# Attention followed by a gated unit: the spatial bias moved from TensorE matmuls to a VectorE add, and the spatial blocks dealt among the blocks of u

## The chip, the cores and the metric

The kernel runs on one core of one Trainium2 chip. Its time is the device time of one execution, in microseconds (us). A core has several engines that run their own instruction streams in order and wait for each other on semaphores. In the profile they are called PE (TensorE, matmuls), PEld (the weight loads of TensorE, which overlap its matmuls), DVE (VectorE), ACT (ScalarE), POOL (GpSimd) and SP (SyncE, which issues most DMAs).

## The reference

Attention with 16 query heads on 4 key heads (batch 8, sequence 384, head size 64) makes x of shape 8 x 384 x 1024. A gated unit follows. All inputs and the output are float32.

```
h = np.maximum(x @ w_in, 0.0)                  # 1024 -> 1024
u, v = h[..., :512], h[..., 512:]
v_n = (v - mean(v)) / np.sqrt(var(v) + 1e-06)  # over the last axis
v_s = np.einsum('ts,bsd->btd', w_spatial, v_n) + b_spatial[None, :, None]
gated = u * v_s
out = gated @ w_out                            # 512 -> 1024
```

The spatial product mixes the 384 positions of the sequence; `b_spatial` has one value for each position t. In the kernel's layout for `v_s` the columns d are on partitions and t runs along the row, so the bias is a row of 384 values that is the same on every partition.

## The kernel before

The work is written out as one order of instructions for each engine. A main loop goes over steps n, 18 for each batch. In a step the attention of batch b is issued: `scores(n)` (tile `sc`, two matmuls of 64 x 512 each, then the exponential on ACT into `aT`) and `weigh` (12 matmuls into `av`, then on DVE the reciprocal `r` and the product `x`, lines 273 and 275; there is one `av` buffer in PSUM, so that each group of `av` waits for the `x` of the one before). DMA loads, casts on POOL and transposes stand in a table `todo` by step. The loads and the transposing DMAs are issued on SP's queue.

Beside the attention of batch b runs the gated unit of batch b-1. `gated_unit(b)` is a Python generator: it issues matmuls and yields their column count after each. `run_fill` takes from it until the columns of this step's share have been issued: `COLS` divided by 18, with `COLS` the columns of one unit (line 397). So PE's order is fixed: in each step attention first, then a share of the unit. The unit of batch b starts at step 18(b+1)+2; that of the last batch (b = 7) runs after all attention, with nothing beside it. "Unit b" below means the call `gated_unit(b)`.

A unit has these parts in order:

- `pv` (line 311): three blocks of 8 matmuls with 512 columns, for the half v. DVE takes each from PSUM with a ReLU (`vr`, line 321), then `stats` and `mv` (lines 323, 324).
- `pu` (line 333): four blocks (m = 0 to 3) of 8 matmuls with 384 columns, for the half u. ACT takes each out with a ReLU as `uT` (line 341). Behind block 0 ACT computes `rstd` (lines 343, 344). Behind block 1 DVE computes `nmr` (line 346) and POOL the three normalised blocks `vn` (line 351), 128 x 512 each.
- `psp` (lines 363 and 366): four spatial blocks. Each starts with one matmul of `ones_b` with `bias_b`, which puts the bias into PSUM (float32 split into two float16 rows, 0 and 32 of `bias_b`; all other rows are zero), then three matmuls with the three `vn`. DVE multiplies the block by `uT` into `gT` (line 374).
- `po` (line 381): six blocks of 4 matmuls with 512 columns; the four take `gT` blocks 0 to 3 as weights in that order. DVE and ACT copy them to `osb` (line 390), SP stores them.

All PSUM blocks of the unit come from one pool, `ps_ck`, with three buffers. The bias is loaded by `load_b` (line 402) and made ready by `prep_spatial` (line 405, three POOL operations on one partition).

Of the kernel before, what the change touches and what calls it, by code (L numbers as in the profile page):

```python
# [9 lines left out]
FP32 = mybir.dt.float32  # L10
FP16 = mybir.dt.float16
AF = mybir.ActivationFunctionType
ALU = mybir.AluOpType
# [4 lines left out]
def kernel(  # L18
# [16 lines left out]
    nc = tc.nc  # L35
    P = 128
    B, HQ, S, D = q.shape
# [3 lines left out]
    DH = DFF // 2  # L41
    NT = S // P
    NB = DM // P
    NM = DH // P
    G = HQ // HKV
    assert (HQ, HKV, S, D, DM, DFF) == (16, 4, 384, 64, 1024, 1024)
    scale = D ** -0.5
# [5 lines left out]
    cst = ctx.enter_context(tc.tile_pool(name="cst", bufs=1))  # L53
# [3 lines left out]
    moe = ctx.enter_context(tc.tile_pool(name="moe", bufs=2))  # L57
# [34 lines left out]
    def load_q0(j, lo, hi, eng):  # L92
# [18 lines left out]
            name=nc.get_next_instruction_name(), act_func_set_id=set_id, ins=[], outs=[]  # L111
# [41 lines left out]
    eps_t = cst.tile([P, 1], FP32, name="eps_t")  # L153
    nc.vector.memset(eps_t, 1e-6)
    v1 = [cst.tile([P, HKV, NT, VW], FP16, name=f"v1_{i}") for i in range(2)]
    for i in range(2):
        nc.gpsimd.memset(v1[i][:, :, :, D:VW], 1.0)
    ones_b = cst.tile([P, P], FP16, name="ones_b")
    nc.gpsimd.memset(ones_b, 0.0)
    nc.gpsimd.memset(ones_b[0:1, :], 1.0)  # L160
    nc.gpsimd.memset(ones_b[32:33, :], 1.0)
    bias_b = cst.tile([P, S], FP16, name="bias_b")
    nc.gpsimd.memset(bias_b, 0.0)


    k16s, q16s = {}, {}
# [115 lines left out]
    def x_tile(b):  # L282
        if b not in xts:
            xts[b] = att.tile([P, NT, NB, P], FP16, name=f"xt_{b}", tag="xt")
        return xts[b]
# [17 lines left out]
    def gated_unit(b):  # L303
        xt = x_tile(b)
        last = b == B - 1
        mv = small.tile([P, NT, 2], FP32, name=f"mv_{b}", tag="mv")
        v_r, v_n = [], []
        for st in range(NT):
            pv = ps_ck.tile([P, 512], FP32, name=f"pv_{b}_{st}", tag="ck")
            for kt in range(NB):  # L310
                nc.tensor.matmul(  # L311
                    pv,
                    xt[:, st, kt],
                    w_in16[:, kt, DH:DFF],
                    start=(kt == 0),
                    stop=(kt == NB - 1),
                )
                if kt < NB - 1:
                    yield 512
            vr = moe.tile([P, DH], FP32, name=f"vr_{b}_{st}", tag="vr", bufs=4)  # L320
            nc.vector.tensor_scalar(vr, pv, 0.0, None, op0=ALU.max)  # L321
            stats = small.tile([P, 6], FP32, name=f"stats_{b}_{st}", tag="stats")
            nc.vector.bn_stats(stats, vr)  # L323
            nc.vector.bn_aggr(mv[:, st, :], stats)
            v_r.append(vr)
            yield 512
        rstd = small.tile([P, NT], FP32, name=f"rstd_{b}", tag="rstd")
        nmr = small.tile([P, NT], FP32, name=f"nmr_{b}", tag="nmr")
        uT = moe.tile([P, NM, S], FP16, name=f"uT_{b}", tag="uT")
        for m in range(NM):  # L330
            pu = ps_ck.tile([P, 512], FP32, name=f"pu_{b}_{m}", tag="ck")
            for kt in range(NB):
                nc.tensor.matmul(  # L333
                    pu[:, 0:S].rearrange("p (t s) -> p t s", t=NT),
                    w_in16[:, kt, m * P : (m + 1) * P],
                    xt[:, :, kt],
                    start=(kt == 0),
                    stop=(kt == NB - 1),
                )
                yield S  # L340
            nc.scalar.activation(uT[:, m, :], pu[:, 0:S], AF.Relu)  # L341
            if m == 0:
                nc.scalar.activation(rstd, mv[:, :, 1], AF.Ln, bias=eps_t)
                nc.scalar.activation(rstd, rstd, AF.Exp, scale=-0.5)
            if m == 1:
                nc.vector.scalar_tensor_tensor(  # L346
                    nmr, mv[:, :, 0], -1.0, rstd, op0=ALU.mult, op1=ALU.mult
                )
                for st in range(NT):
                    vn = moe.tile([P, DH], FP16, name=f"vn_{b}_{st}", tag="vn", bufs=6)  # L350
                    nc.gpsimd.tensor_scalar(  # L351
                        vn,
                        v_r[st],
                        rstd[:, st : st + 1],
                        nmr[:, st : st + 1],
                        op0=ALU.mult,
                        op1=ALU.add,
                    )
                    v_n.append(vn)
        gT = moe.tile([P, NM, S], FP16, name=f"gT_{b}", tag="gT")  # L360
        for m in range(NM):
            psp = ps_ck.tile([P, 512], FP32, name=f"psp_{b}_{m}", tag="ck")
            nc.tensor.matmul(psp[:, 0:S], ones_b, bias_b, start=True, stop=False)  # L363
            yield S
            for st in range(NT):
                nc.tensor.matmul(  # L366
                    psp[:, 0:S],
                    v_n[st][:, m * P : (m + 1) * P],
                    wsT16[:, st, :],
                    start=False,  # L370
                    stop=(st == NT - 1),
                )
                yield S
            nc.vector.tensor_tensor(gT[:, m, :], psp[:, 0:S], uT[:, m, :], ALU.mult)  # L374
        rows = out[b].rearrange("(p t) d -> p t d", t=NT)
        for tt in range(NT):
            osb = ops.tile([P, DM], FP32, name=f"osb_{b}_{tt}", tag="osb")
            for half in range(2):
                po = ps_ck.tile([P, 512], FP32, name=f"po_{b}_{tt}_{half}", tag="ck")
                for m in range(NM):  # L380
                    nc.tensor.matmul(  # L381
                        po,
                        gT[:, m, tt * P : (tt + 1) * P],
                        w_out16[:, m, half * 512 : (half + 1) * 512],
                        start=(m == 0),
                        stop=(m == NM - 1),
                    )
                    yield 512
                cols = slice(half * 512, (half + 1) * 512)
                (nc.scalar.copy if half else nc.vector.tensor_copy)(osb[:, cols], po)  # L390
                if last:
                    nc.sync.dma_start(rows[:, tt, cols], osb[:, cols])
            if not last:
                nc.sync.dma_start(rows[:, tt, :], osb)

    HV = NB * 512
    COLS = NT * HV + NM * NB * S + NM * (NT + 1) * S + NT * 2 * NM * 512


    b32 = cst.tile([1, S], FP32, name="b32")  # L400

    def load_b():
        nc.sync.dma_start(b32, moe_b_spatial.rearrange("(a s) -> a s", a=1))

    def prep_spatial():
        lo32 = cst.tile([1, S], FP32, name="lo32")
        bp = b32.rearrange("a (p t) -> a t p", t=NT)
        hi = bias_b[0:1, :].rearrange("a (t p) -> a t p", t=NT)
        nc.gpsimd.tensor_copy(hi, bp)
        nc.gpsimd.tensor_tensor(lo32.rearrange("a (t p) -> a t p", t=NT), bp, hi, ALU.subtract)  # L410
        nc.gpsimd.tensor_copy(bias_b[32:33, :], lo32)

    def load_ws():
        t = cst.tile([P, NT, S], FP32, name="ws32")
# [53 lines left out]
    at(12, load_w_in, 1, 0)  # L468
    at(13, load_ws)
    at(13, load_b)  # L470
    at(13, load_w_out, 0)
    at(14, k_transposes, 1, 0, by_dve)
# [47 lines left out]
    def run_fill(cols):  # L520
        nonlocal owed
        owed = owed + cols if fill else 0.0
        while fill and owed > 0:
            try:
                owed -= next(fill[0])
            except StopIteration:
                fill.pop(0)

    early = 0
    for n in range(total + 6):  # L530
        for f, args in todo.pop(n, []):
            f(*args)
        if n + 1 < NU:
            scores(n + 1)
        elif n >= NU and n % 2 == 0 and n < total:
            scores(n)
            scores(n + 1)
        for hh in range(2):
            b, r = divmod(n - 3 - hh, NU)
            if n >= 3 + hh and r % 3 == 0 and b < B:  # L540
                weigh(b, r // 3, hh)
        if n == 13:
            fill.append(gated_unit(0))
        if n >= 2 * NU + 2 and (n - 2) % NU == 0 and (n - 2) // NU <= B:
            fill.append(gated_unit((n - 2) // NU - 1))
        if n < NU + 3:
            if 13 <= n and early < 2 * HV:
                c = min(768, 2 * HV - early)
                early += c
                run_fill(c)  # L550
        else:
            run_fill((COLS - (early if n < 2 * NU + 2 else 0)) / (NU if n >= 2 * NU + 2 else NU - 1))
    for g in fill:
# [31 lines left out]
```

## Time and profile before

| What | us |
| --- | --- |
| median of 3 runs | 267.28 |
| lowest, highest | 263.93, 268.06 |
| the profiled execution | 264.56 |
| its span, first to last instruction | 262.6 |
| PE busy | 243.8 |
| ACT busy | 169.0 |
| DVE busy | 143.7 |
| POOL busy | 73.0 |
| 32 bias matmuls, mean of one (with latency) | 0.325 |
| 96 spatial matmuls, mean of one (with latency) | 0.326 |
| gT, mean of one of 32 | 0.556 |

The profile is of one execution. The duration of a matmul there includes its latency; matmuls overlap, and the distance from one start to the next is the time that PE is taken. In the groups of instructions a row gives line, engine, operation, output and inputs with shapes, count, then busy time and mean ns of one, then the idle time of the engine just ahead of them and who ended it. In the timeline a row gives start, duration, engine, line, operation, and a count where neighbours were merged; idle time ahead is in square brackets. In a table of stages a row gives the stretch, its length, busy time of PE, PEld, DVE, ACT and POOL with counts, the granted TensorE clock as a share of full speed, DMA share and GB/s.

### The profile page before, as it was taken

To read this page: it belongs to the slowest core of one execution; us is meant where nothing else is said; L and a number is where in the kernel's file an instruction comes from. 1 tells how busy PE (TensorE), PEld (TensorE's weight loads), DVE (VectorE), ACT (ScalarE), POOL (GpSimd) and SP (SyncE) were. 2 spreads that over 40 slices of the span, in tenths; PEclk is the share of its full clock that TensorE was granted. 3 is DMA by queue.
4 is the path that set the end of the run, shared out by engine and by line. 5 is a ranking of instruction groups with operands and counts; after the bars stand their busy time and mean duration, and the time that the engine had idled before them with its cause. 6 is when DMAs were issued, how large, how long until landed. Compare 5 with 4: busy or idle time off the path is not lost.

```text
span 262.6 us, 5743 instructions
## 1 busy us (share of the span) xinstructions
PE 243.8 (93%) x2325; PEld 123.5 (47%) x2325; DVE 143.7 (55%) x372; ACT 169.0 (64%) x218; POOL 73.0 (28%) x112
## 2 busy tenths in 40 slices
PE   1776879999999999999999999999999998999994
PEld 1343435554455444554455445544455445544551
DVE  3257577455563647374654556364736465465642
ACT  2668346777768675868677776867586865862222
POOL 2446697614103330316013510333030000300120
PEclk9999799999999999999999999999999999999999
DMA  7999798399909995599739990999465340005006
GB/s 188 330 353 353 258 388 262 74 266 252 287 6 204 299 295 69 104 286 284 202 64 200 275 313 21 179 325 224 151 116 113 111 171 2 0 2 240 2 0 240
DMA packets 76715, 49.32 MB, mean 188 GB/s; under 512 B 45969, under 2 KB 70546, under 8 KB 76690
## 3 DMA queue, kind: packets, MB, share of 16 engines
q1 hardware_dynamic: 75650, 48.70, 70.3%
q8 instruction: 18, 0.29, 0.5%
q10 hardware_dynamic: 1040, 0.26, 0.4%
q14 instruction: 7, 0.06, 0.1%
HBM read 25.76 MB, written 12.58 MB: 146 GB/s over the span
## 4 chain that ended last, share of the span: by engine, by line
PE 83%; DVE 6%; DMA 5%; issue 1%; ACT 1%; SPq 1%; POOL 0%; DVEq 0%
PE pu L333 16%; PE av L263 15%; PE po L381 15%; PE pv L311 14%; PE sc L249 13%; PE psp L366 6%; DMA q<-in_q_dram 3%; DMA xt<-x 2%; DVE x L275 2%; PE psp L363 2%; PE xps L291 1%; PE qps L216 1%; DVE w_in L134 1%; DVE r L273 1%; ACT osb L390 1%
## 5 line engine op out<-in xcount | busy, mean ns | idle before, releaser
L256 ACT ACTIVATE aT<-sc 128x1024 f16<-128x1024 f32 x144 | 139.7, 1022 | 64.5 <-PE sc L249 64.4
L263 PEld LDWEIGHTS <-aT 128*128 128x128 f16 x1152 | 44.7, 98 | 33.8 <-issue 7.5
L263 PE MATMUL av<-v,aT 128*128 128x65 f16 x1152 | 53.2, 195 | 4.1 <-DVE x L275 3.8
L273 DVE RECIPROCAL r<-av 128x4 f32<-128x4 f32 x96 | 17.0, 177 | 65.6 <-PE av L263 65.6
L351 POOL TENSOR_SCALAR vn<-vr,rstd,nmr 128x512 f16<-128x512 f32 x24 | 18.2, 773 | 116.5 <-DVE nmr L346 94.3
L311 PE MATMUL pv<-w_in,xt 128*128 128x512 f16 x192 | 47.9, 380 | 0.3 <-DVE osb L390 0.2
L249 PE MATMUL sc<-qT,kT 64*128 64x512 f16 x288 | 46.8, 394 | 1.5 <-ACT aT L256 0.7
L381 PE MATMUL po<-w_out,gT 128*128 128x512 f16 x192 | 47.8, 379 | 0.4 <-ACT osb L390 0.3
L333 PE MATMUL pu<-xt,w_in 128*128 128x384 f16 x256 | 47.8, 326 | 0.0
L275 DVE TENSOR_TENSOR x<-av,r 128x256 f16<-128x256 f32 x96 | 40.7, 424 | 3.3
L188 POOL CAST q<-q 128x768 f16<-128x768 f32 (+1 forms) x32 | 24.8, 803 | 20.0 <-DMA q<-in_q_dram 14.5
L333 PEld LDWEIGHTS <-w_in 128*128 128x128 f16 x256 | 22.9, 97 | 15.5 <-issue 3.0
L311 PEld LDWEIGHTS <-xt 128*128 128x128 f16 x192 | 16.6, 97 | 18.3 <-issue 3.1
L381 PEld LDWEIGHTS <-gT 128*128 128x128 f16 x192 | 16.7, 97 | 16.1 <-DVE gT L374 1.7
L374 DVE TENSOR_TENSOR gT<-psp,uT 128x384 f16<-128x384 f32 x32 | 17.7, 556 | 10.2 <-PE psp L366 9.5
L366 PE MATMUL psp<-wsT,vn 128*128 128x384 f16 x96 | 22.2, 326 | 0.0
L249 PEld LDWEIGHTS <-kT 64*128 64x128 f16 x288 | 9.5, 94 | 26.9 <-issue 24.9
L390 ACT COPY osb<-po 128x512 f32<-128x512 f32 x24 | 14.1, 589 | 12.4 <-PE po L381 12.4
L321 DVE TENSOR_SCALAR vr<-pv 128x512 f32<-128x512 f32 x24 | 16.6, 691 | 9.0 <-PE pv L311 8.3
L341 ACT ACTIVATE uT<-pu 128x384 f16<-128x384 f32 x32 | 15.6, 493 | 9.0 <-PE pu L333 9.0
L390 DVE COPY osb<-po 128x512 f32<-128x512 f32 x24 | 16.5, 687 | 6.1 <-PE po L381 6.0
L323 DVE BATCH_NORM_STATS2 stats<-vr 128x6 f32<-128x512 f32 x24 | 16.7, 694 | 0.8
(45 smaller groups left out, 105.3 us busy)
## 6 DMA issues: line engine op xcount, KB each, us to landing
q<-in_q_dram SPq DMA_DIRECT2D x14, 768.0 KB, 7.9
out_dram<-osb SPq DMA_DIRECT2D x21, 512.0 KB, 3.9
wi<-in_moe_w_in_dram SPq DMA_DIRECT2D x4, 1024.0 KB, 9.4
v<-in_v_dram SPq DMA_DIRECT2D x8, 384.0 KB, 9.0
k<-in_k_dram SPq DMA_DIRECT2D x7, 384.0 KB, 4.6
wo<-in_moe_w_out_dram SPq DMA_DIRECT2D x2, 1024.0 KB, 6.9
out_dram<-osb SPq DMA_DIRECT2D x6, 256.0 KB, 2.0
q<-in_q_dram SPq DMA_DIRECT2D x2, 512.0 KB, 7.6
```

The source lines that it names most:

```text
L188: eng.tensor_copy(q16s[b, j][:, lo:hi, :, hh, :], src[:, hh, lo:hi])
L249: nc.tensor.matmul(sc[:, hh], kTs[b][half, j, t * P : (t + 1) * P], qTs[b, j][half, qt], start=True, stop=True,)
L256: nc.scalar.activation(aTs[b, m][:, t], sc, AF.Exp, scale=scale)
L263: nc.tensor.matmul(av[:, i, :], aTs[b, m][:, t, hh, i * P : (i + 1) * P], v1[b % 2][:, 2 * j + hh, t, 0 : D + 1], start=(t == 0), stop=(t ...
L273: nc.vector.reciprocal(r, av[:, :, D : D + 1])
L275: nc.vector.tensor_tensor(x16s[b][:, qt, blk : blk + 2].rearrange("p k (i d) -> p (k i) d", i=2), av[:, :, 0:D], r.to_broadcast([P, G, D]) ...
L311: nc.tensor.matmul(pv, xt[:, st, kt], w_in16[:, kt, DH:DFF], start=(kt == 0), stop=(kt == NB - 1),)
L333: nc.tensor.matmul(pu[:, 0:S].rearrange("p (t s) -> p t s", t=NT), w_in16[:, kt, m * P : (m + 1) * P], xt[:, :, kt], start=(kt == 0), stop ...
L351: nc.gpsimd.tensor_scalar(vn, v_r[st], rstd[:, st : st + 1], nmr[:, st : st + 1], op0=ALU.mult, op1=ALU.add,)
L366: nc.tensor.matmul(psp[:, 0:S], v_n[st][:, m * P : (m + 1) * P], wsT16[:, st, :], start=False, stop=(st == NT - 1),)
L381: nc.tensor.matmul(po, gT[:, m, tt * P : (tt + 1) * P], w_out16[:, m, half * 512 : (half + 1) * 512], start=(m == 0), stop=(m == NM - 1),)
L390: (nc.scalar.copy if half else nc.vector.tensor_copy)(osb[:, cols], po)
```

## The change

The bias is loaded to all 128 partitions and kept as float32 (`bias_bc`). A spatial block has only its three matmuls. DVE first adds the bias to the block from PSUM into a float32 tile `vs` in SBUF, and multiplies `vs` by `uT` into `gT` with a second operation. The order of the blocks changes: u 0, u 1, the normalisation (`normal`), u 2, spatial 0, u 3, spatial 1, 2, 3. `nmr` and `vn` are issued after the yield that follows block 1 of u. `COLS` loses the columns of the bias matmuls: 41472 for 43008, 2304 for 2389 a step.

```diff
-    ones_b = cst.tile([P, P], FP16, name="ones_b")
...
-    bias_b = cst.tile([P, S], FP16, name="bias_b")
-    nc.gpsimd.memset(bias_b, 0.0)
+    bias_bc = cst.tile([P, S], FP32, name="bias_bc")
...
+        def u_block(m):
             pu = ps_ck.tile([P, 512], FP32, name=f"pu_{b}_{m}", tag="ck")
             for kt in range(NB):
...
-                yield S
+                if kt < NB - 1:
+                    yield S
             nc.scalar.activation(uT[:, m, :], pu[:, 0:S], AF.Relu)
...
+            yield S
+
+        def normal():
+            nc.vector.scalar_tensor_tensor(
+                nmr, mv[:, :, 0], -1.0, rstd, op0=ALU.mult, op1=ALU.mult
+            )
+            for st in range(NT):
...
+        def spatial_block(m):
             psp = ps_ck.tile([P, 512], FP32, name=f"psp_{b}_{m}", tag="ck")
-            nc.tensor.matmul(psp[:, 0:S], ones_b, bias_b, start=True, stop=False)
-            yield S
             for st in range(NT):
                 nc.tensor.matmul(
                     psp[:, 0:S],
                     v_n[st][:, m * P : (m + 1) * P],
                     wsT16[:, st, :],
-                    start=False,
+                    start=(st == 0),
                     stop=(st == NT - 1),
                 )
-                yield S
-            nc.vector.tensor_tensor(gT[:, m, :], psp[:, 0:S], uT[:, m, :], ALU.mult)
+                if st < NT - 1:
+                    yield S
+            vs = moe.tile([P, S], FP32, name=f"vs_{b}_{m}", tag="vs")
+            nc.vector.tensor_tensor(vs, psp[:, 0:S], bias_bc, ALU.add)
+            nc.vector.tensor_tensor(gT[:, m, :], vs, uT[:, m, :], ALU.mult)
+            yield S
+
+        yield from u_block(0)
+        nc.scalar.activation(rstd, mv[:, :, 1], AF.Ln, bias=eps_t)
+        nc.scalar.activation(rstd, rstd, AF.Exp, scale=-0.5)
+        yield from u_block(1)
+        normal()
+        yield from u_block(2)
+        yield from spatial_block(0)
+        yield from u_block(3)
+        for m in range(1, NM):
+            yield from spatial_block(m)
...
-    COLS = NT * HV + NM * NB * S + NM * (NT + 1) * S + NT * 2 * NM * 512
+    COLS = NT * HV + NM * NB * S + NM * NT * S + NT * 2 * NM * 512
...
-    b32 = cst.tile([1, S], FP32, name="b32")
+    b32 = cst.tile([P, S], FP32, name="b32")
...
-        nc.sync.dma_start(b32, moe_b_spatial.rearrange("(a s) -> a s", a=1))
+        nc.sync.dma_start(b32, moe_b_spatial.partition_broadcast(P))
...
-        nc.gpsimd.tensor_tensor(lo32.rearrange("a (t p) -> a t p", t=NT), bp, hi, ALU.subtract)
-        nc.gpsimd.tensor_copy(bias_b[32:33, :], lo32)
+        nc.gpsimd.tensor_copy(
+            bias_bc.rearrange("a (t p) -> a t p", t=NT), b32.rearrange("a (p t) -> a t p", t=NT)
+        )
```

More of the change, by code (lines that the diff above doesn't have):

```diff
@@ L157 @@
         nc.gpsimd.memset(v1[i][:, :, :, D:VW], 1.0)
-    ones_b = cst.tile([P, P], FP16, name="ones_b")
-    nc.gpsimd.memset(ones_b, 0.0)
-    nc.gpsimd.memset(ones_b[0:1, :], 1.0)
-    nc.gpsimd.memset(ones_b[32:33, :], 1.0)
-    bias_b = cst.tile([P, S], FP16, name="bias_b")
-    nc.gpsimd.memset(bias_b, 0.0)
+    bias_bc = cst.tile([P, S], FP32, name="bias_bc")
     k16s, q16s = {}, {}
@@ L329, in gated_unit @@
         uT = moe.tile([P, NM, S], FP16, name=f"uT_{b}", tag="uT")
-        for m in range(NM):
+        gT = moe.tile([P, NM, S], FP16, name=f"gT_{b}", tag="gT")
+        def u_block(m):
             pu = ps_ck.tile([P, 512], FP32, name=f"pu_{b}_{m}", tag="ck")
@@ L339, in gated_unit @@
                 )
-                yield S
+                if kt < NB - 1:
+                    yield S
             nc.scalar.activation(uT[:, m, :], pu[:, 0:S], AF.Relu)
[L342 to L347, printed above, removed]
-                )
[L349 to L361, printed above, removed]
+            yield S
[4 more added lines that the diff above has]
+            for st in range(NT):
+                vn = moe.tile([P, DH], FP16, name=f"vn_{b}_{st}", tag="vn", bufs=6)
+                nc.gpsimd.tensor_scalar(
+                    vn,
+                    v_r[st],
+                    rstd[:, st : st + 1],
+                    nmr[:, st : st + 1],
+                    op0=ALU.mult,
+                    op1=ALU.add,
+                )
+                v_n.append(vn)
+        def spatial_block(m):
             psp = ps_ck.tile([P, 512], FP32, name=f"psp_{b}_{m}", tag="ck")
-            nc.tensor.matmul(psp[:, 0:S], ones_b, bias_b, start=True, stop=False)
-            yield S
             for st in range(NT):
@@ L396 @@
     HV = NB * 512
-    COLS = NT * HV + NM * NB * S + NM * (NT + 1) * S + NT * 2 * NM * 512
-    b32 = cst.tile([1, S], FP32, name="b32")
+    COLS = NT * HV + NM * NB * S + NM * NT * S + NT * 2 * NM * 512
+    b32 = cst.tile([P, S], FP32, name="b32")
     def load_b():
-        nc.sync.dma_start(b32, moe_b_spatial.rearrange("(a s) -> a s", a=1))
+        nc.sync.dma_start(b32, moe_b_spatial.partition_broadcast(P))
     def prep_spatial():
[L406 to L409, printed above, removed]
-        nc.gpsimd.tensor_tensor(lo32.rearrange("a (t p) -> a t p", t=NT), bp, hi, ALU.subtract)
-        nc.gpsimd.tensor_copy(bias_b[32:33, :], lo32)
+        nc.gpsimd.tensor_copy(
+            bias_bc.rearrange("a (t p) -> a t p", t=NT), b32.rearrange("a (p t) -> a t p", t=NT)
+        )
     def load_ws():
```

## The prediction

> **What bounds the kernel now.** I read the page's first part for the engines, then busy time by stage, then the groups of the lines that the diff touches, then the timeline of one unit (unit b is the call gated_unit(b); its work on PE is dealt among the attention of batch b+1, and the last unit runs alone), and the granted clock last.
>
> ```profile
> PE 243.8 (93%) x2325; PEld 123.5 (47%) x2325; DVE 143.7 (55%) x372; ACT 169.0 (64%) x218; POOL 73.0 (28%) x112
> ```
> ```profile
> 181.50:210.10 28.60, 28.60 (x278) 14.02 (x276) 15.88 (x41) 20.64 (x28) 2.28 (x3) 1.00 0.54 139
> ```
> The second line is unit 5: length, then PE, PEld, DVE, ACT and POOL busy, clock, DMA. PE is busy all of it, DVE little over half. A busy PE need not be at its peak, so I check by spacing. From its pv at 181.53 to that of unit 6 at 210.11 are 28.58 us. In the last unit 32 pu matmuls take 5.36 us, the last of them 0.33, so one of 384 columns takes (5.36-0.33)/31 = 0.162; 24 pv take 5.34, so one of 512 takes 0.216. Four sc take 0.54 (193.65 to 194.19) and twelve av 0.38 (194.19 to 194.57). A unit has 48 matmuls of 512 (10.4), 32 pu (5.2), 16 psp with the bias (2.6), 9 groups of sc (4.9) and 12 of av (4.6): 27.7 of 28.58. So PE's order of work is the clock of units 0 to 7; about 0.9 us a unit is spare, and a PE wait is added in full.
>
> ```profile
> L351 POOL TENSOR_SCALAR vn<-vr,rstd,nmr 128x512 f16<-128x512 f32 x24 | 18.2, 773 | 116.5 <-DVE nmr L346 94.3
> L374 DVE TENSOR_TENSOR gT<-psp,uT 128x384 f16<-128x384 f32 x32 | 17.7, 556 | 10.2 <-PE psp L366 9.5
> L366 PE MATMUL psp<-wsT,vn 128*128 128x384 f16 x96 | 22.2, 326 | 0.0
> L323 DVE BATCH_NORM_STATS2 stats<-vr 128x6 f32<-128x512 f32 x24 | 16.7, 694 | 0.8
> ```
> The third line is the one to look at: psp never waits for vn today. The timeline of unit 5 shows how closely that is so (start, duration, and idle time in brackets):
>
> ```profile
> 193.65 0.61 PE L249 MATMUL sc<-qT,kT 64*128 64x512 f16 x4
> ...
> 193.88 0.16 DVE L346 SCALAR_TENSOR_TENSOR nmr<-mv,rstd 128x3 f32<-128x3 f32 x1 [0.46 <-ACT rstd L344]
> ...
> 194.19 0.54 PE L263 MATMUL av<-v,aT 128*128 128x65 f16 x12
> 194.22 2.28 POOL L351 TENSOR_SCALAR vn<-vr,rstd,nmr 128x512 f16<-128x512 f32 x3 [13.14 <-DVE nmr L346]
> ...
> 194.57 2.27 PE L333 MATMUL pu<-xt,w_in 128*128 128x384 f16 x13
> 194.77 0.18 DVE L273 RECIPROCAL r<-av 128x4 f32<-128x4 f32 x1 [0.72 <-PE av L263]
> 194.99 0.42 DVE L275 TENSOR_TENSOR x<-av,r 128x256 f16<-128x256 f32 x1
> ...
> 197.85 0.33 PE L363 MATMUL psp<-bias_b,ones_b 128*128 128x384 f16 x1
> ...
> 202.40 0.46 PEld L381 LDWEIGHTS <-gT 128*128 128x128 f16 x3 [0.19 <-DVE gT L374]
> ```
> The three vn end at 196.50, and PE comes to psp at 197.85: 1.35 us of cover, made of pu blocks 2 and 3 with sc and av between. At the other end the last gT of a unit is just in time (0.19).
>
> **The change part by part.**
>
> *Bias matmuls go.* 32 x 0.162 = 5.2 us of PE time, 0.65 a unit, all on the path.
>
> *Where psp block 0 and nmr come to stand.* In the built order of the changed kernel, units 1 to 6 run on PE: 6 pu, sc, av, 8 pu (block 2), 3 psp (block 0), pu block 3 with sc and two av, psp 1 to 3, 2 po, av, 2 po. The fill deals 2304 columns a step, not 2389, and block 1 of u ends with a step; nmr is therefore issued a step later and on DVE stands behind r and x of that av, where before it stood ahead of them. Counted from the av at 194.19 (in the changed kernel it comes 2 pu earlier, which shifts all that follows alike): x ends at 195.41, nmr (0.16) at 195.61, POOL starts 0.18 later as before (194.04 to 194.22), at 195.8, and at 0.765 each the vn end at 196.56, 197.33 and 198.1. PE reaches psp 0 at 194.57 + 8 x 0.162 = 195.87. Its third matmul can start at about 198.15 and not at 196.19: 1.95 us lost. Behind it in PE's queue stand all pu, sc and av; nothing is run in their place. Bounds: 1.75, if x overlaps nmr and nothing passes between the engines; 2.2, if POOL's result takes another 0.2 to reach PE. Six units x 1.95 = 11.7. In unit 0 block 1 ends a matmul before a step's end, so that nmr stays ahead of r, and sc and two av lie between: vn end at 51.6 (49.31 + 2.28), PE reaches psp 0 at about 52.8. Nothing lost there. Unit 6 has the x transposes of the last batch and their copies between; I take it as the others.
>
> *Second DVE operation.* The add reads PSUM and a second operand as gT does: 0.556. The product reads SBUF alone; the nearest row is stats, 694 for 512 elements, so 694 - 128/0.96 = 0.56 for 384. With 0.03 between operations (vr to stats) a block costs 1.18 where it cost 0.59. The Trainium skill, "VectorE: DVE Perf Modes", section on the errata for SBUF-source operations, tables 58 cycles plus one per element from SBUF to SBUF: an estimate of 0.46 us by that page. The row of stats disagrees with it, and the row decides; by the page a unit's three blocks would lose 0.3 us less.
> PE makes psp 1 to 3 with one sc group between, in about 2.1 us; DVE needs 3.5, and r and x (0.63) come first. I continue unit 5 from psp 0's end at 198.3: psp 1 leaves PE at 201.4, psp 3 at 203.05, two po at 203.5, av at 203.85. DVE: vs 1 starts at 201.65, and three pairs end at 202.8, 204.0 and 205.2. The third and fourth po want gT 2 and gT 3; the fourth starts at 205.2 where it could have at 204.1. So 1.1 us lost; bounds 0.7 (product at 0.42, by DVE's cast of q, 290 ns for 256 elements from SBUF) and 1.2 (a gap of 0.06 instead of 0.03). Six units: 6.6. Behind the third pair on DVE stand r and x of that av, and the next av on PE waits for them; the two po and sc between (0.97) cover their 0.65. In unit 0 only one sc group stands between psp 3 and the po: r and x, vs 2, gT 2, vs 3 and gT 3 end about 3 us after psp 3, less sc 0.54 and three po 0.65: 1.9 lost.
>
> *The last unit*, with nothing beside it:
>
> ```profile
> 248.66 2.28 POOL L351 TENSOR_SCALAR vn<-vr,rstd,nmr 128x512 f16<-128x512 f32 x3 [22.20 <-PE pu L333]
> ...
> 252.50 1.86 DVE L374 TENSOR_TENSOR gT<-psp,uT 128x384 f16<-128x384 f32 x3 [0.16 <-PE psp L366]
> ...
> 254.41 4.22 PEld L381 LDWEIGHTS <-gT 128*128 128x128 f16 x21 [0.56 <-DVE gT L374]
> ```
> Block 2 of u ends at 249.62; psp 0 could end at 250.1 and must wait for the third vn (250.94), to 251.2: 1.1 lost. Then u 3 to 252.5 and psp 1 to 253.0, out at 253.15; three pairs on DVE end at 256.5, where the last gT ended at 254.36. The fourth po moves from 254.41 to 256.5: 2.1 later, net of this unit's bias matmuls.
>
> *Costed at nothing:* the load of the bias on 128 rows (hidden by 13 us between its issue and its use; uncovered it would hold unit 0's first add); one POOL copy for three operations of 0.69, 1.01 and 0.50 (POOL next waits 0.75 for q anyway); the memsets, under POOL's first wait for v; SP's new order, where the last x transpose of a batch passes the last store (PE's waits for xt are 0.8 in all, so a gain of at most that). ACT gets the same operations.
>
> *Sum.* -0.65 x 7 + 11.7 + 6.6 + 1.9 + 2.1 = +17.7. The profiled execution took 264.56 (span 262.6, so 2.0 around it): 282.3, **282 us**. Its time lies 2.7 under the median, 267.28, of runs from 263.93 to 268.06; from the median the sum gives 285.0.
>
> **The rivals.**
> *Faster: the waits are hidden.* If nmr ran where it does now, and DVE caught up under the attention, PE keeps the 5.2 us: 259.4. For it: DVE is 55% busy and POOL 28%. Against it: those are averages, and cover between nmr and psp falls from 13 pu, sc and av to 8 pu. It decides if both waits together stay under 0.65 us a unit.
> *Only one wait is real*, say the pairs on DVE (or vn at a third of its size): 282.3 - 8 = about 274. For it: today's 0.19 us is the only wait of this kind. Against: vn's 2.28 us is fixed, and PE's 1.3 us in front of psp 0 can be counted.
> *The clock falls as well.*
>
> ```profile
> 26.00:27.00 1.00, 0.00 (x0) 0.00 (x0) 0.97 (x4) 0.68 (x1) 0.24 (x1) 1.00 1.05 391
> 27.00:28.00 1.00, 0.54 (x13) 0.49 (x14) 0.40 (x1) 0.00 (x0) 0.00 (x0) 1.00 1.04 385
> 28.00:29.00 1.00, 1.00 (x10) 0.55 (x7) 0.91 (x3) 0.00 (x0) 0.93 (x2) 0.71 1.07 406
> 29.00:30.00 1.00, 1.00 (x5) 0.23 (x4) 0.48 (x2) 0.21 (x1) 1.00 (x3) 0.50 0.86 343
> ```
> PE waited 2.17 us, and from about 28.5 to 31.9 the clock was half. Gaps of 0.6 to 0.9 before it did nothing. Each wait for vn is 1.95 us, in three pieces with a psp matmul between. If each cost 3.4 us at half clock, 1.7 us would be lost per unit, 10 in six: 288 with some, 292 with all. The Trainium skill, "TensorE: Matmul & The Clock Gate", section "HAM oscillation — how this bites in real kernels", allows idle gaps up to about 3.4 us, so by that page none would fall; the trace does not agree, since 2.17 was enough. I hold the pieces for enough work, but not safely.
>
> **How the numbers follow.** Forecast 0.70, own range 277 to 287 (bounds of vn: -1.2 to +1.5; of DVE: -2.4 to +0.6; start from 264.56 or from the median). Clock 0.14, at 287 to 294. One wait 0.08, at 272 to 277. Little changed 0.04, faster 0.04. The range, 273 to 290, leaves out the faster cases and the upper half of the clock's. About 2% is what a measurement of this kernel tells from no change: faster 0.04, same 0.06 (with the low end of one wait), slower 0.90.
>
> **What would show it.** The psp group on PE with some 12 us idle, released by POOL vn; weight loads of po waiting for DVE gT for some 10; vs near 0.56 and gT near 0.56; a unit of about 31.0 us where 28.58 stands; no psp from bias_b. Wrong if: vn starts under 0.5 us after the end of u block 1; or the clock row shows more than one dip after 33 us.

## The result, and the profile after

The changed kernel takes 282.62 us (median of 4 runs, 279.59 to 287.58), the kernel before beside it 266.01 (4 runs, 263.93 to 268.06): ratio 1.061, 95% interval 1.046 to 1.077. The ratio leaves out 287.58 and 268.06, each more than 1.5% above the shortest run of its kernel. The profiled execution took 279.59, its span is 277.8.

The engines on the page of the changed kernel, to be set beside the same line of before:

```profile
PE 244.7 (88%) x2293; PEld 119.8 (43%) x2293; DVE 159.8 (58%) x404; ACT 170.5 (61%) x218; POOL 73.7 (27%) x106
```

PE has 32 matmuls fewer, yet its share falls from 93% to 88% and the span grows by 15.2: PE waits. Its groups say for whom (busy and mean ns, then idle time ahead and its releaser):

```profile
L361 PE MATMUL psp<-wsT,vn 128*128 128x384 f16 x96 | 22.1, 328 | 8.2 <-POOL vn L348 8.1
L391 PE MATMUL po<-w_out,gT 128*128 128x512 f16 x192 | 49.7, 380 | 8.3 <-DVE gT L372 7.6
L391 PEld LDWEIGHTS <-gT 128*128 128x128 f16 x192 | 16.5, 97 | 27.0 <-DVE gT L372 12.3
L371 DVE TENSOR_TENSOR vs<-psp,bias_bc 128x384 f32<-128x384 f32 x32 | 17.7, 554 | 20.3 <-PE psp L361 20.3
L372 DVE TENSOR_TENSOR gT<-vs,uT 128x384 f16<-128x384 f32 x32 | 18.6, 581 | 2.8
```

Before, psp had no idle time, as the prediction shows, and po 0.4:

```profile
L381 PE MATMUL po<-w_out,gT 128*128 128x512 f16 x192 | 47.8, 379 | 0.4 <-ACT osb L390 0.3
```

The timeline of unit 5, where the first wait is made:

```profile
203.33 0.54 PE L258 MATMUL av<-v,aT 128*128 128x65 f16 x12
...
203.71 1.46 PE L330 MATMUL pu<-xt,w_in 128*128 128x384 f16 x8
...
204.12 0.42 DVE L270 TENSOR_TENSOR x<-av,r 128x256 f16<-128x256 f32 x1
204.46 0.15 DVE L343 SCALAR_TENSOR_TENSOR nmr<-mv,rstd 128x3 f32<-128x3 f32 x1
204.79 2.27 POOL L348 TENSOR_SCALAR vn<-vr,rstd,nmr 128x512 f16<-128x512 f32 x3 [14.06 <-DVE nmr L343]
...
205.62 0.34 PE L361 MATMUL psp<-wsT,vn 128*128 128x384 f16 x1 [0.45 <-POOL vn L348]
...
206.37 0.34 PE L361 MATMUL psp<-wsT,vn 128*128 128x384 f16 x1 [0.42 <-POOL vn L348]
...
207.12 0.34 PE L361 MATMUL psp<-wsT,vn 128*128 128x384 f16 x1 [0.41 <-POOL vn L348]
```

The eight pu would let the third psp start at 203.71 + 10 x 0.162 = 205.33; it starts at 207.12, one POOL block after the other: 1.8 us lost. The idle time drawn ahead of the three is only 1.28, since a matmul is drawn with its latency (0.34 where it takes PE 0.162) and so covers part of each wait. nmr stands right behind x on DVE. The second wait, 6 us later in the same unit:

```profile
211.82 0.55 DVE L371 TENSOR_TENSOR vs<-psp,bias_bc 128x384 f32<-128x384 f32 x1
...
212.47 0.56 DVE L372 TENSOR_TENSOR gT<-vs,uT 128x384 f16<-128x384 f32 x1
...
212.95 0.55 DVE L371 TENSOR_TENSOR vs<-psp,bias_bc 128x384 f32<-128x384 f32 x1
...
213.09 0.39 PE L391 MATMUL po<-w_out,gT 128*128 128x512 f16 x1
213.60 0.56 DVE L372 TENSOR_TENSOR gT<-vs,uT 128x384 f16<-128x384 f32 x1
...
214.22 0.82 PE L391 MATMUL po<-w_out,gT 128*128 128x512 f16 x3 [0.74 <-DVE gT L372]
```

A pair takes 1.13 on DVE. The fourth po could start 0.216 behind the third, at 213.31, and starts at 214.22 with the last gT: 0.9 lost. Together 2.7, less 0.65 for the bias matmuls: 2.05 a unit. The chain of work (start, length, work) gives the length of units: before, the first pv of units 1, 5, 6 and 7; then the changed kernel's:

```profile
67.38 1.19 PE pv L311 x5
...
181.59 1.18 PE pv L311 x5
...
210.18 1.19 PE pv L311 x5
...
240.55 5.34 PE pv L311 x24
```
```profile
67.75 1.19 PE pv L306 x5
...
191.17 1.19 PE pv L306 x5
...
221.87 1.18 PE pv L306 x5
...
253.40 5.34 PE pv L306 x24
```

28.59 became 30.70. From unit 1 to unit 7 the chain runs from 67.38 to 240.55 before and from 67.75 to 253.40 after: 12.5 us of the 15.2 are in units 1 to 6. The last unit, to the end of the span, went from 22.05 to 24.4.

### The profile page after: what moved, and what is told of

Read it like the earlier page. It is cut to its first block, busy times and chain, and to the rows that moved or that the text cites. A ratio compares the mean times of both kernels' runs of the same rounds, so it can differ in the third digit from the quotient of the medians.

```text
span 277.8 us, 5707 instructions
## 1 busy us (share of the span) xinstructions
PE 244.7 (88%) x2293; PEld 119.8 (43%) x2293; DVE 159.8 (58%) x404; ACT 170.5 (61%) x218; POOL 73.7 (27%) x106
## 4 chain that ended last, share of the span: by engine, by line
PE 69%; DVE 17%; POOL 6%; issue 3%; DMA 2%; ACT 1%; SPq 1%; POOLq 1%; DVEq 0%
PE pv L306 15%; PE av L258 14%; PE po L391 13%; PE sc L244 12%; PE pu L330 12%; POOL vn L348 5%; DVE gT L372 5%; DVE vs L371 4%; DVE x L270 4%; DMA q<-in_q_dram 2%; DVE r L268 2%; PE psp L361 1%; PE qps L211 1%; PE xps L286 1%; DVE w_in L134 1%
## 5 line engine op out<-in xcount | busy, mean ns | idle before, releaser
L258 PEld LDWEIGHTS <-aT 128*128 128x128 f16 x1152 | 44.7, 99 | 33.8 <-issue 9.6
L391 PE MATMUL po<-w_out,gT 128*128 128x512 f16 x192 | 49.7, 380 | 8.3 <-DVE gT L372 7.6
L330 PE MATMUL pu<-xt,w_in 128*128 128x384 f16 x256 | 50.3, 326 | 0.0
L306 PE MATMUL pv<-w_in,xt 128*128 128x512 f16 x192 | 48.5, 379 | 0.2 <-DVE osb L400 0.2
L183 POOL CAST q<-q 128x768 f16<-128x768 f32 (+1 forms) x32 | 27.1, 874 | 17.9 <-DMA q<-in_q_dram 16.6
L371 DVE TENSOR_TENSOR vs<-psp,bias_bc 128x384 f32<-128x384 f32 x32 | 17.7, 554 | 20.3 <-PE psp L361 20.3
L330 PEld LDWEIGHTS <-w_in 128*128 128x128 f16 x256 | 22.8, 97 | 14.8 <-issue 3.0
L339 ACT ACTIVATE uT<-pu 128x384 f16<-128x384 f32 x32 | 15.8, 493 | 12.5 <-PE pu L330 12.5
L400 ACT COPY osb<-po 128x512 f32<-128x512 f32 x24 | 14.2, 592 | 10.1 <-PE po L391 10.1
L372 DVE TENSOR_TENSOR gT<-vs,uT 128x384 f16<-128x384 f32 x32 | 18.6, 581 | 2.8
```

The source lines that it names most:

```text
L183: eng.tensor_copy(q16s[b, j][:, lo:hi, :, hh, :], src[:, hh, lo:hi])
L258: nc.tensor.matmul(av[:, i, :], aTs[b, m][:, t, hh, i * P : (i + 1) * P], v1[b % 2][:, 2 * j + hh, t, 0 : D + 1], start=(t == 0), stop=(t ...
L306: nc.tensor.matmul(pv, xt[:, st, kt], w_in16[:, kt, DH:DFF], start=(kt == 0), stop=(kt == NB - 1),)
L330: nc.tensor.matmul(pu[:, 0:S].rearrange("p (t s) -> p t s", t=NT), w_in16[:, kt, m * P : (m + 1) * P], xt[:, :, kt], start=(kt == 0), stop ...
L371: nc.vector.tensor_tensor(vs, psp[:, 0:S], bias_bc, ALU.add)
L372: nc.vector.tensor_tensor(gT[:, m, :], vs, uT[:, m, :], ALU.mult)
```

## The experiments

The theory: two waits of PE, each with a cause of its own (vn late behind nmr's new place; pairs on DVE ahead of po), on a path where PE's order is the clock. The rivals: only one of the two; DVE's load as such, through other waits; a PE with spare time; the clock. Times below are medians, each with the ratio to the kernel before on the same chip.

**The bias by matmul, in the changed order.** In the changed kernel, with the bias loaded and prepared as in the kernel before:

```diff
+            nc.tensor.matmul(psp[:, 0:S], ones_b, bias_b, start=True, stop=False)
...
-            vs = moe.tile([P, S], FP32, name=f"vs_{b}_{m}", tag="vs")
-            nc.vector.tensor_tensor(vs, psp[:, 0:S], bias_bc, ALU.add)
-            nc.vector.tensor_tensor(gT[:, m, :], vs, uT[:, m, :], ALU.mult)
+            nc.vector.tensor_tensor(gT[:, m, :], psp[:, 0:S], uT[:, m, :], ALU.mult)
```

> The changed kernel's order and steps, but the bias again by one matmul ahead of each spatial block (not counted in the fill) and one DVE product. Theory (two waits, each with its own cause): psp block 0 still waits for the third vn, 1.8 - 0.16 = 1.64 us in units 1 to 6 and about 1 us in the last, and the wait of po for gT is gone: before plus 10.8, about 277 where before is 266. Rival (the second DVE operation is all the cost): as before, 266. Rival (the order is all the cost): as the changed kernel, 283.

Measured: 274.8 (before 264.69), ratio 1.038 (1.032 to 1.044): 10.1 more than before, 10.8 expected. Its groups:

```profile
L367 PE MATMUL psp<-wsT,vn 128*128 128x384 f16 x96 | 24.5, 329 | 6.9 <-POOL vn L353 6.7
L395 PE MATMUL po<-w_out,gT 128*128 128x512 f16 x192 | 47.8, 379 | 0.4 <-ACT osb L404 0.3
```

The wait for vn stands alone; that for gT is gone. So the order by itself costs some 10 us, with DVE's work as it was.

**The added DVE operation, in the old order.** In the kernel before: no bias matmul, `COLS` with NT for NT + 1, and

```diff
-            nc.vector.tensor_tensor(gT[:, m, :], psp[:, 0:S], uT[:, m, :], ALU.mult)
+            vs = moe.tile([P, S], FP32, name=f"vs_{b}_{m}", tag="vs")
+            nc.vector.tensor_tensor(vs, psp[:, 0:S], bias_bc, ALU.add)
+            nc.vector.tensor_tensor(gT[:, m, :], vs, uT[:, m, :], ALU.mult)
```

> The order of blocks of the kernel before (u 0 to 3, then spatial 0 to 3), no bias matmuls, the bias by the added DVE operation. Theory: psp does not wait for vn (4 more pu, sc, av and 4 more pu lie between); four DVE pairs of 1.13 us follow each other behind psp 0, so the fourth po waits about 2.1 us; less 0.65 of bias matmuls is +1.5 in each of units 0 to 6 and +1.7 in the last: before plus 12, about 278. Rival (the wait for vn is all the cost, DVE hides): 266 - 5 = 261.

Measured: 280.9 (before 264.69), ratio 1.054 (1.046 to 1.062); 16.2 more by the medians, where 12 was expected.

```profile
L376 PE MATMUL po<-w_out,gT 128*128 128x512 f16 x192 | 53.1, 395 | 14.1 <-DVE gT L369 12.9 <-DVE vs L368 0.6 <-DVE xt L287 0.3
L359 PE MATMUL psp<-wsT,vn 128*128 128x384 f16 x96 | 19.3, 326 | 0.0
```

Now the wait for vn is gone and that for gT is larger, as four pairs stand in a row. The operation alone does harm as well; dealing one block among those of u does shorten this wait, but pays with the other. Most of the 4 us beyond the forecast are the clock: in the profiled execution the mean granted clock is 0.976, with three stretches of 3.41 us at half clock right behind long waits and one in the start. Busy time in the stretches (length, PE, PEld, DVE, ACT, POOL; then clock, DMA share, GB/s):

```profile
59.43:62.85 3.42, 1.03 (x15) 0.62 (x16) 2.51 (x4) 0.61 (x1) 2.58 (x3) 1.00 1.20 307
62.85:66.26 3.41, 3.41 (x25) 1.19 (x22) 1.21 (x3) 1.00 (x2) 0.94 (x2) 0.50 1.14 165
```
```profile
182.31:185.73 3.42, 1.84 (x17) 0.72 (x15) 3.11 (x7) 1.32 (x2) 1.93 (x2) 1.00 1.11 326
185.73:189.14 3.41, 3.26 (x20) 1.21 (x21) 1.32 (x5) 1.22 (x2) 1.60 (x2) 0.50 1.32 240
```

At half clock two po matmuls of 512 columns start 0.427 apart where they start 0.216 apart otherwise, so 3.41 us of matmuls do the work of 1.7. In this profile units 2 and 4, with such a stretch, are 31.7 us long from pv to pv, units 1, 3 and 5, without one, 29.8 to 29.9. Three stretches are 5.1, and 16.2 - 5.1 = 11.1, near the 12. The same kernel ran once more without any such stretch (last experiment): 277.13, which is 12.7 more than before.

**nmr ahead of r and x.** In the changed kernel:

```diff
             nc.scalar.activation(uT[:, m, :], pu[:, 0:S], AF.Relu)
+            if m == 1:
+                normal()
             yield S
...
         yield from u_block(1)
-        normal()
```

> The changed kernel with one move: nmr and vn are issued ahead of the yield that ends block 1 of u, so that nmr stands on DVE ahead of r and x of that av and not behind them. Theory: nmr starts when rstd is there (203.0 in the unit that begins at 191.1) and not at 204.46, the third vn ends at about 205.7 and not 207.07, and psp 0 loses 0.4 us and not 1.8; units 1 to 6 gain 1.4 each: 8.4 less than the changed kernel, about 274. The wait of po for gT stays at 0.9. Rival (POOL's 2.3 us and not nmr's place set the end of vn): under 2 us of change, 281.

Measured: 272.94 (before 264.69), ratio 1.031 (1.026 to 1.036), against 1.061 of the changed kernel. That is 8.3 more than before beside it where the changed kernel was 16.6 more: 8 us less, 8.4 expected. The nearest two groups:

```profile
L363 PE MATMUL psp<-wsT,vn 128*128 128x384 f16 x96 | 20.9, 327 | 1.7 <-POOL vn L350 1.5
L392 PE MATMUL po<-w_out,gT 128*128 128x512 f16 x192 | 51.3, 390 | 8.7 <-DVE gT L374 8.1 <-ACT osb L401 0.3
```

Half of the loss hung on one instruction of 0.15 us that was issued a step later, and on the three POOL operations behind it. The other wait did not move.

**No bias at all**, in the order of before; the bias is left out (with `COLS` as in the changed kernel).

```diff
-            nc.tensor.matmul(psp[:, 0:S], ones_b, bias_b, start=True, stop=False)
-            yield S
```

> The order of the kernel before without any bias (it is left out: no bias matmuls, no add). It measures what the removed matmuls are worth where nothing is put in their place. Theory (PE's order is the clock): 32 x 0.162 = 5.2 less than before, 261. Rival (PE has spare time that swallows it): 264 to 266.

Measured: 259.59 (before 264.69), ratio 0.982 (0.974 to 0.989): 5.1 less, 2.9 to 6.9 by the interval. PE has no slack that swallows them; this is what the change had to win.

**The first two po blocks side by side.** In the changed kernel, for tt = 0:

```diff
-            for half in range(2):
...
+                for m in range(NM):
+                    for half in group:
+                        nc.tensor.matmul(
+                            pos[half],
...
```

> The changed kernel, with the first two po blocks of a unit issued m by m side by side (two PSUM blocks open), so that six matmuls and not three stand ahead of the first that wants gT block 3. Theory: the wait of po for gT falls by 3 x 0.216 = 0.65 us in each of the eight units; the wait of psp for vn stays 1.8: 5.2 less than the changed kernel, about 277 where before is 266. Rival (the wait for gT is not on the path, another is behind it): under 1.5 us of change.

Measured: 277.02 (before 264.02), ratio 1.047 (1.040 to 1.054), against 1.061 (1.046 to 1.077). That is 13.0 more than the kernel before beside it where the changed kernel was 16.6 more: 3.6 less, 5.2 expected. The two intervals overlap, but the profile is clear: PE's idle time ahead of po falls from 8.3 to 3.2 while that ahead of psp stays at 8.2, and units 2, 3 and 5 take 30.15 us from pv to pv where they took 30.70. Part of the gain comes back as waits of av for x, one of 0.2 to 0.5 in each of units 1 to 6, where the changed kernel has none. So this wait was on the path too.

**Both waits covered**: the two moves above, and spatial block 0 behind the fourth matmul of u block 3 (`u_block` takes a generator that it runs there).

```diff
         yield from u_block(2)
-        yield from spatial_block(0)
-        yield from u_block(3)
+        yield from u_block(3, spatial_block(0))
```

> The changed kernel with three moves: nmr and vn issued ahead of the yield of u block 1, spatial block 0 put in the middle of u block 3 (behind 4 of its 8 matmuls), and the first two po blocks side by side. Theory: no wait for vn in units 0 to 6, some 0.3 us of waiting for gT left in each of units 1 to 6, so that the 0.65 us of the bias matmuls are hardly won: within 2 us of before, 263 to 266. Rival (the second DVE operation costs time elsewhere, through r and x and the av that wait for them): 268 or more.

Measured: 266.03 (12 runs; before 264.02), ratio 1.007 (1.003 to 1.010). All but 2 us of the loss is gone, but the 5.1 are not won. PE's waits in this kernel (total, times, longest):

```profile
PE av L258 <- DVE x L270: 4.2, 11, 1.2
...
PE po L398 <- DVE vs L375: 1.0, 3, 0.6
PE po L398 <- DVE gT L376: 0.7, 2, 0.5
```

Units 1 to 6 together take 172.5 us, 173.2 in the kernel before and 168.8 without any bias. What is left of the wait for the pairs (the last two lines) is part of that. The next in line is the other: r and x of the attention stand behind the pairs on DVE, and with one buffer for av PE waits for x. Of the 4.2 us only 1.6 are of this kind, one wait of 0.2 to 0.6 in each of units 1 to 6, where the kernel before has none; the rest stands in the start, where before has 3.8 as well. That was the rival of this experiment, true at a smaller size; the time lies at the upper edge of the forecast.

**And one product on POOL.**

```diff
-            nc.vector.tensor_tensor(gT[:, m, :], vs, uT[:, m, :], ALU.mult)
+            (nc.gpsimd if m == 1 else nc.vector).tensor_tensor(gT[:, m, :], vs, uT[:, m, :], ALU.mult)
```

> As the kernel with the covered waits, and the product of spatial block 1 with u on POOL, which then is idle. DVE's row behind psp 1 shortens from 6 operations to 5, 0.59 us. Theory: the rest of the wait for gT goes in units 1 to 6, and unit 0 and the last gain 0.6 each: 3 to 4 less than the kernel with the covered waits, about 261. Rival (POOL and DVE hold each other up when both read SBUF, as gT took 1.01 us beside a cast of q of 1.15 us in one unit of the changed kernel): no gain, and gT rows of DVE with durations over 0.7 us.

Measured: 265.21 (before 264.02), ratio 1.002 (0.999 to 1.005). 0.8 less than with both waits covered, and not 3 to 4.

```profile
L376 DVE TENSOR_TENSOR gT<-vs,uT 128x384 f16<-128x384 f32 x24 | 16.4, 683 | 1.9
L376 POOL TENSOR_TENSOR gT<-vs,uT 128x384 f16<-128x384 f32 x8 | 7.3, 914 | 32.6 <-DVE vs L375 32.6
```

The mean of gT on DVE is 683 where it was 580 with both waits covered; of its 24 products nine took 0.73 to 0.97, each beside a POOL operation, eight of them casts of k and q. PE's waits for the pairs fall from 1.7 to 0.7, but x comes later, and the wait for it grows from 4.2 to 6.2:

```profile
PE av L258 <- DVE x L270: 6.2, 11, 1.2
```

The rival of this experiment holds in part. No version here that has the bias beats the kernel before.

**Matmuls into the waits.** The kernel with the old order and the added operation, with eight matmuls of zero weights a unit that add nothing to the sum; and that kernel once more beside it.

```diff
+                    if tt == 0 and half == 0 and m > 0:
+                        for _ in range((2, 2, 4)[m - 1]):
+                            nc.tensor.matmul(po, zeros, w_out16[:, 0, 0:512], start=False, stop=False)
```

> The kernel with the old order and the added DVE operation a second time, beside the one with fillers. As before, 278 to 283, with a mean clock of 0.976 to 0.988 (two to four stretches of 3.4 us at half clock).

> The same, with eight matmuls of zero weights added into the first po block of each unit (two ahead of its second matmul, two ahead of its third, four ahead of its fourth; they add zero to the sum). 8 x 0.216 = 1.73 us of PE work a unit lies in the waits for gT, which are 2.15 a unit. Theory (the clock goes by the share of each 3.41 us in which PE is busy): the waits stay, the dips beside them go, and the time falls by what the dips cost, 1.7 us each, 3 to 5 in all, to about 277, with more work on PE; mean clock 0.993 or more. Rival (the dips come from something else, or only one idle stretch counts): time up by up to 2 us for fillers that do not fit, and the clock as without them.

Measured beside each other (before 264.46): without fillers 280.88 (277.13 to 281.78, 6 runs), with them 278.29 (277.79 to 279.09, 5 runs), ratio to before 1.054 (1.051 to 1.058). Without, the mean clock of the runs was 1.0, 0.994, 0.982 (three) and 0.976, and the time followed it: 277.1 and 278.3 at the two highest, 280.1 to 281.8 at the others. With fillers it was 0.994 to 1.0 in every run; of the ten runs without, the four above included, eight lie at 0.988 or lower. So the dips (stretches at half clock) go when PE is kept busy, though gT comes no sooner, and 14 us of PE work (64 x 0.216) cost 0.7 to 2.0 against the run that had no dip anyway. Only the long runs are shortened: the three shortest without fillers have a median of 278.26. The gain, 2.6 for 3 to 5, is smaller than expected, since not every run without fillers has three dips.

## Why the prediction was right

- **The bias matmuls, -5.2.** Shown: 5.1 where nothing replaces them.
- **Where nmr comes to stand, 1.95 a unit.** Right in mechanism, with 1.8 in the trace: nmr starts 0.08 ahead of the drawn end of x (204.46 and 204.54), where 0.04 behind it was allowed, and PE starts on a block some 0.07 behind POOL (205.62 for a block that ends at 205.55). Moving nmr, with the vn behind it, shows that it is this wait, and on the path: 8 us.
- **The second DVE operation, 0.56.** gT's median is 0.559. The Trainium skill, "VectorE: DVE Perf Modes", section on the errata for SBUF-source operations, has beside the table that was set against the row a formula for a float32 tensor_tensor, elements plus 151 cycles at 0.96 GHz: an estimate of 0.557 for 384 by that page, which the trace bears out (here uT is float16); its table (0.46) it does not.
- **The wait for gT, 1.1 a unit.** The trace has 0.9. The mis-sized term is the pair, 1.18, which is 1.13 (211.82 to 212.95): vs starts 0.08 ahead of the drawn end of gT, and gT 0.10 behind that of vs, so that a pair takes 0.02 more than its two operations, where 0.06 was allowed. Three pairs make 0.15 of it; the rest is not traced.
- **The sum.** Units 1 to 6 were to lose 2.4 each and lost 2.08, 12.5 for 14.4. The last unit lost 2.35 for 2.1; the forecast's own working, three pairs of 1.18 from 253.15, gives 256.66 and not 256.5, and so 2.25. In unit 0 the third and fourth po start at 58.54 and 59.67, 0.5 and 0.9 late: 1.45 for 1.9. What the start and unit 0 lost in all is not separated: the profile of before has a half-clock stretch at 28.4 in the start, which that of after has not, so the 0.37 us by which unit 1 starts later hide some 1.7. Against the median beside it the change costs 16.6; the forecast was 17.7. That 282 and 282.62 lie so close is partly luck: the sum was 1.1 too large, and it was added to 264.56, which is 1.45 below the median beside the change.
- **The rival that PE keeps the 5.2.** It needed both waits under 0.65 together; the ratio of 1.007 with both covered shows that even then what is left of the waits, and x behind the pairs, take nearly all of it.
- **The rival of one wait.** Each stands by itself: the order alone costs 10.1, the added operation alone 12.7 where no dip falls in.
- **The rival of the clock** is real, but did not decide here. It had been argued from one idle stretch of 2.17 us, and the pieces of psp were held for enough work. In the profiled execution no stretch of 3.41 us comes under the line that the last section gives (lowest in units 1 to 6: 0.61 busy, at 180.19; 0.57 once in the start and once in the last unit); two of the four runs of the changed kernel show a mean clock of 0.988, which two such stretches at half clock would make.

## What to carry to other kernels

When an engine's order is the clock, count the cover in instructions: what stands on that engine between the event that starts a side chain and the first use of its result, against the length of that chain, with the queue of each engine in it. A move that looks free on an engine that is half idle can put a short instruction behind two others in its queue; here that was half of the loss. And once a wait is long enough for the clock, it costs more than itself.

## What the runs showed of the hardware

**The clock goes by a share, not by one gap.** The half-clock stretches last 3.413 us, and their starts within a run lie on a grid of that length (62.85, 124.29 and 185.73 are 18 steps apart). With the grid laid through all eleven profiles of this case, from the first clock record of each (14.8 to 33.8 us into the span) to its last whole stretch, each of the ten grid stretches in which PE was busy for 0.54 of the time or less was followed by one at half clock, and none of the other 779, with 0.554 or more, was. Busy is meant as the profile draws it, with the latency of the matmuls. Two lines near it, of the changed kernel, with no dip behind them:

```profile
26.59:30.00 3.41, 1.93 (x24) 1.18 (x25) 2.63 (x9) 1.05 (x2) 1.70 (x4) 1.00 1.04 394
180.19:183.60 3.41, 2.07 (x20) 0.99 (x19) 3.17 (x7) 1.70 (x2) 2.84 (x4) 1.00 1.16 309
```

1.93 of 3.41 is 0.57; the stretch from 182.31 above has 1.84 of 3.42, 0.54, and the next is at half clock. The longest wait alone does not decide: PE was idle for 1.80 us in one piece just ahead of 28.05 in the changed kernel with no dip behind it, and no wait that touches the stretch from 182.31 is longer than 0.74. Whether the same wait costs 1.7 us more thus depends on how it falls on the grid, which is one reason why runs of one kernel differ. It is not the only one: two runs of the changed kernel with a mean clock of 1.0 took 279.59 and 282.32. The Trainium skill, "TensorE: Matmul & The Clock Gate", section "Part 1: The HAM clock gate", says that the window is free-running and 3413 ns long, which the traces bear out, and asks for an idle window; here 46% of idle time in several pieces was enough.

**DVE and POOL hold each other up over SBUF.** In unit 4 of the changed kernel:

```profile
179.73 1.93 POOL L183 CAST q<-q 128x768 f16<-128x768 f32 x2 [1.47 <-DMA q<-in_q_dram]
179.96 1.01 DVE L372 TENSOR_TENSOR gT<-vs,uT 128x384 f16<-128x384 f32 x1
180.89 0.55 DVE L371 TENSOR_TENSOR vs<-psp,bias_bc 128x384 f32<-128x384 f32 x1
```

gT, with both inputs in SBUF, takes 1.01 and not 0.56; vs, with one input in PSUM, keeps its 0.55; the two casts take 1.93 where two took 1.60 before. The one that comes second is the longer one: this gT starts inside the first cast, which takes its usual 0.83, and the second cast, which starts inside gT, takes 1.15. Of the 32 products of this profile only three are longer than 0.56 (0.59, 0.80 and 1.01). But unit 4, which holds two of them, is 31.4 us long from pv to pv where units 1, 2, 3 and 5 are 30.6 to 30.7. The Trainium skill, "SBUF — State Buffer", section "SBUF: two separate sides", has it that a DVE operation with two SBUF inputs and a POOL operation that reads SBUF lock each other out; the trace agrees. It was not tried by itself.
